# Stationary tiles at other addresses: feed-forward weights in steps of 16 bytes, one buffer of X and of g 64 bytes further

## The chip, the core and the metric

The kernel runs on one core of a Trainium2 chip. The metric is device time in microseconds (us) of one execution. TensorE (PE in the rows) multiplies: a *weight load* (PEld) brings a stationary tile of up to 128 x 128 values from SBUF into the array, and a matmul then streams a moving tile from SBUF through it. VectorE (DVE), ScalarE (ACT) and GpSimd (POOL) do the elementwise work; SyncE (SP) issues transfers.

## The reference, cut to what matters

```python
X = np.fft.rfft(x, axis=1)                         # x: (8, 3072, 256)
Yr = Xr @ w_r - Xi @ w_i + b_r                     # complex channel mixing, 256 x 256
Yi = Xr @ w_i + Xi @ w_r + b_i
Y  = soft_threshold(Yr, 0.01) + 1j * soft_threshold(Yi, 0.01)
y  = np.fft.irfft(Y, n=3072, axis=1)
h  = y.reshape(-1, 256) @ w_in                     # 256 -> 2048
g  = np.where(h >= 1, h, np.where(h <= -1, 0, (h + 1) ** 2 / 4))
out = g @ w_out                                    # 2048 -> 256
```

## The kernel before, in words

Everything is one core's program, written out in a fixed order under `tc.manual_schedule()`; no scheduler moves anything. It has two stages.

**FFT and mixing** (the loop over `u`, 96 steps and a tail). The transform is done by matmuls with tables (`stage1`, `stage2`, `stage3`, `stage4`). The channel mixing between them is L319, `mixed`: the stationary tile is a 128 x 128 piece of X (`Xdh`, `Xdl`, `Xh`, `Xl`: the high and low part of a value, so that three single-pass products stand for one in full precision), the moving tile is a 128 x 256 mixing matrix (`wm_..`). Each step has 18 such matmuls, 96 x 18 = 1,728 in all, and eight steps have 6 more with the narrow `e0` tiles. Each X tile has two buffers, taken in turn from step to step. `stage2` (L251) has `z_first` (first batch) or `zin` (the others) as its stationary tile and the table `t_sb` as its moving one.

**Feed-forward** (the loop over `n`, 256 units; unit n is pair p = n mod 8 of block i = n // 8). In each unit
- L582, `product`, called seven times with three matmuls each: the stationary tile is a 128 x 128 slice of `win` (high or low part, block p), the moving one 128 x 384 of the rows `oph`/`opl`. The seven products are the first matrix product done with seven sub-products in place of eight;
- L638, `down`, eight times with three matmuls each: the stationary tile is a slice of `wout` (block 2p + f), the moving one 128 x 384 of the gated values `gh`/`gl`.

That is 256 x 21 = 5,376 and 256 x 24 = 6,144, together 11,520 matmuls of one form, and runs of `product` and `down` alternate: product 1 and 2, `down` of the unit before last, product 6, `down`, products 5, 7 and 4, `down` of the last unit with f = 1, product 3, `down`, `down` with f = 0. Along this order the stationary tile passes nine times in a unit from one block of weights to another (product to `down`, `down` to product, or from f = 1 to f = 0).

Between these stand `stage4` calls (L500) in every eighth unit, after which the feed-forward stream starts anew.

Where tiles lie: a pool places its tiles one behind the other. Of an address only the remainder modulo 128 bytes is spoken of below. Before the change, each moving tile of L319, L582 and L638 (`wm`, `oph`, `opl`, `gh`, `gl`) and each stationary one (X, `win`, `wout`) begins at a multiple of 128 bytes, and so does each 512-byte row slice of them that one matmul reads, since their sizes are multiples of 128 bytes (`win` of a block 7 x 128 x 4 = 3,584; `wout` of a block 2,048; an X tile 1,024 or 2,048; `g` 3,072). Other remainders occur in the program before in one matmul form that also occurs at remainder 0: `zin` begins 32 bytes past a multiple of 128, `z_first` at a multiple, and `t_sb` at a multiple.

Of the kernel before, what the change touches and what calls it, by code (L numbers as in the profile page):

```python
# [11 lines left out]
F32R = mybir.dt.float32r  # L12
# [4 lines left out]
P = 128  # L17
R1 = 48
R2 = 64
# [84 lines left out]
def tile_fft_mix_moe(  # L104
# [3 lines left out]
    B, S, D = x.shape  # L108
    DFF = w_in.shape[1]
    NF = DFF // P  # L110
    ND = D // P
# [4 lines left out]
    NP = NF // 2  # L116
# [4 lines left out]
    TH = QT * JH // 2  # L121
# [10 lines left out]
    keep = ctx.enter_context(tc.tile_pool(name="keep", bufs=1, side="left"))  # L132
    banks = lambda name: tc.alloc_tile_pool(name=name, bufs=1, space=bass.MemoryType.PSUM, reuse_waits="tile")
    pools = {"ps": banks("psum")}
    dram = ctx.enter_context(tc.tile_pool(name="dram", bufs=1, space=bass.MemoryType.DRAM))
    fold = left("fold")
    mixing = left("mixing")
# [8 lines left out]
    zh, uh = ([a and a.rearrange("(r h) j d -> h r j d", h=2) for a in y_d] for y_d in (z_d, u_d))  # L146


    win = [[keep.tile([P, 7, P], F32R, name=f"win{k}{p}") for p in range(NP)] for k in "hl"]
    z_first = keep.tile([P, G, D], F32, tag="wout", name="z_first")  # L150
    c2_sb = keep.tile([P, R1], F32, name="c2_sb")
    half = keep.tile([P, 1], F32, name="half")
# [20 lines left out]
    def load_x(h):  # L173
        b, m = divmod(h, NJ)
        xin[h] = first_st.tile([P, JT, D], F32, tag="xin", bufs=AHEAD, name="xin")
        if b == 0:
            nc.gpsimd.memset(xin[h][: HP - R1], 0.0)
            to = xin[h][HP - R1 : HP + R1].rearrange("p (a j) d -> p a (j d)", a=2)
            rows = x_first[m].rearrange("a k r i e n -> (k r) a (i e n)")
            for part in (slice(0, 1), slice(1, 2)) if m < 2 else (slice(0, 2),):  # L180
                nc.sync.dma_start(to[:, part], rows[:, part])
            return
        for k in range(2):
            nc.sync.dma_start(xin[h][k * HP : k * HP + R1], xh[b, k, :, m * JT : (m + 1) * JT, :])
# [44 lines left out]
    def store_z(h):  # L229
        b, m = divmod(h, NJ)  # L230
        for k in range(2):
            z = zst.pop((h, k))
            for e in range(2):
                j = m * JT + e * HT
                nc.sync.dma_start(zh[b][k, :, j : j + HT, :], z[e * HP : e * HP + R1])


    zin, xp, dp, yp, over, ust, first_col = {}, {}, {}, {}, {}, {}, {}

    def load_z(u):  # L240
        b, v = divmod(u, NU)
        zin[u] = mixing.tile([P, 2, D], F32, tag="zin", bufs=3, name="zin")
        nc.sync.dma_start(zin[u], zg[b][:, 2 * v : 2 * v + 2, :])
# [15 lines left out]
    def both(ps):  # L259
        return (ps[:, :, c].rearrange("p d g s -> p d (g s)") for c in range(2))  # L260

    def split_X_hi(u):
        ps = xp[u]
        _, im = both(ps)
        if u == 0:
            dp[u] = fold.tile([P, 2, D], F32, tag="yb", name="im")[:, :, :P]
        else:
            dp[u] = mixing.tile([P, ND, P], F32, tag="Xd", name="Xd")
        nc.scalar.copy(dp[u], im)
        if u > 0:  # L270
            round_X(u)

    def round_X(u):
        ps = xp[u]
        hi = mixing.tile([P, ND, 2, 2, R2], F32R, tag="Xh", bufs=2, name="Xh")
        nc.scalar.copy(hi, ps)
        xp[u] = ps, hi

# [28 lines left out]

    def split_difference(u):
        dif = dp[u]
        hi, lo = dp[u] = [mixing.tile([P, ND, P], F32R, tag=f"Xd{k}", bufs=2, name=f"Xd{k}") for k in "hl"]  # L310
        nc.scalar.copy(hi, dif)
        return lambda: nc.vector.tensor_tensor(out=lo, in0=dif, in1=hi.bitcast(F32), op=ALU.subtract)

# [15 lines left out]
    def mix_shared(u):  # L329
        ps = yp[u] = pools["ps"].tile([P, 2, D], F32, tag="C", bufs=2, name="ps_mix")  # L330
        mixed(ps[:, 0, :], [(dp.pop(u), "i")], True)
# [51 lines left out]
    def store_u(u):  # L383
        b, v = divmod(u, NU)
        nc.sync.dma_start(ug[b][:, 2 * v : 2 * v + 4, :], ust.pop(u).rearrange("p k g d -> p (k g) d"))
# [15 lines left out]
    def load_weights(step):  # L401
        if step < NW:
            raw = wraw[step] = first_st.tile([P, WC, 2], U32, tag="wraw", bufs=2, name="wraw")
            nc.sync.dma_start(raw.rearrange("p n k -> p (n k)"), weight_source(step).bitcast(U32))
# [160 lines left out]
    ups, snaps, hs, rs, gs, acc, outs = {}, {}, {}, {}, {}, {}, {}  # L565
# [39 lines left out]
    def of(f):  # L605
        return slice(2 * f, 2 * f + 2)
# [10 lines left out]

    def split_hi(n, f):
        if 0 <= n < NUNIT:
            gs[n, f] = [pools["ffg"].tile([P, 2, TH], F32R, tag=f"g{k}{f}", bufs=2, name=f"g{k}") for k in "hl"]  # L620
            nc.scalar.copy(gs[n, f][0], hs[n][:, of(f)])  # L621

    def split_lo(n, f):
# [52 lines left out]
    def halves(u):  # L676

        lo, hi = (min(NH, NJ + (max(0, k - 1) if k <= NJ else NJ + 2 * (k - NJ) // 3)) for k in (u, u + 1))
        return range(lo, hi)

    def load_t(lo, hi, queue=nc.sync):
        queue.dma_start(t_sb[:, lo:hi, :], t_f[:, lo:hi, :])

    def load_ti(u, queue=nc.sync):
        queue.dma_start(ti_sb[:, u], t_i[:, 2 * u : 2 * u + 2, :])

    with tc.manual_schedule():
# [73 lines left out]
        for u in range(UN + 3):  # L761
            odd = u % 2
            due.extend(h for h in halves(u) if h > NX + 1)
            hs_u = due[: 1 if not odd else max(0, len(due) - 1)]
            del due[: len(hs_u)]
            at = lambda lag: 0 <= u - lag < UN
            weights = more_weights if WU <= u < 85 else lambda: None
            while (stored, 0) in zst:
                store_z(stored)
                stored += 1  # L770
            if at(6) and not odd:
                store_u(u - 6)
            if u == NU:
                wout = keep.tile([P, NF, 2, D], F32R, tag="wout", name="wout")
            if 0 < u < NU - 3:
                load_t(2 * u + 6, 2 * u + 8)
            if 0 < u <= NU:
                load_ti(u - 1)
            if u == WU - 1:
                load_weights(0)  # L780
                load_weights(1)
            if u == 10:
                nc.sync.dma_start(c2_sb, c2)
            if NU <= u + 2 < UN:
                assert stored >= NJ * ((u + 2) // NU + 1)
                load_z(u + 2)
            if xs < min(NH, used + AHEAD):
                load_x(xs)
                xs += 1
            if at(2):  # L790
                mix_shared(u - 2)
            if u == 2:
                take_shared(0)
                split_first(0)
            if at(1):
                difference(u - 1)
                rest = split_difference(u - 1)
                if u == 1:
                    round_X(0)
            if at(2) and u > 2:  # L800
                take_shared(u - 2)
            if at(3):
                above(u - 3)
            if at(1):
                if u > 1:
                    split_X_lo(u - 1)
                rest()
                if u == 1:
                    split_X_lo(u - 1)
                    first_col[0] = minus_sum(*first_col[0])  # L810
                else:
                    split_first(u - 1)
            if at(3):
                shrink(u - 3)
            weights()
            if at(5) and odd:
                stage3(u - 5)
            for h in hs_u:
                stage1(h, "AB", [nc.scalar.copy] * 2)
                used += 1  # L820
            if u in U4:
                half4()
            weights()
            if u == UN + 1:
                half4("DD")
            if u < UN:
                stage2(u)
                split_X_hi(u)
            if u == 1:
                stage1(NX + 1, "AB", [nc.scalar.copy] * 2)  # L830
                used += 1
            if at(2):
                mix_rest(u - 2)
                weights()
                add_bias(u - 2)
            if u == U_IN:
                assert not due and stored == NH
                for _ in ws:
                    pass
                first_st.release()  # L840
                pools["in"] = right("in")
                pools["in"].tile([P, 24], F32, name="edge")
                pools["ops0"] = right("ops0")
                for c in range(2):
                    load_u(c)
            if u == UN - 2:
                prep_sums(0)
            for part in {UN - 2: (0,), UN - 1: (1,), UN: (2, 3)}.get(u, ()):
                prep_split_hi(0, part)
                prep_split_lo(0, part)  # L850
# [24 lines left out]
        for n in range(NUNIT):  # L875
            i, p = divmod(n, NP)
# [24 lines left out]
            if n == 0:  # L901
# [3 lines left out]
                c = next(four4)  # L905
# [24 lines left out]
            if n == 0:  # L930
                c = next(four4)
# [27 lines left out]
            if n in four:  # L959
                c = four[n]  # L960
# [5 lines left out]
        n = NUNIT - 1  # L966
# [41 lines left out]
```

## Time and profile before

| | |
|---|---|
| median of 3 runs | 2570.19 us (2569.08 to 2571.77) |
| the profiled execution's own time | 2569.82 us |
| its span, first to last instruction | 2568.0 us |
| mean granted TensorE clock | 0.999 of full speed (2.4 GHz) |
| busy, share of the span | PE 100%, DVE 80%, ACT 66%, POOL 5% |

Matmuls are pipelined, and a matmul's recorded duration runs on while the next one streams. The pace of a run of matmuls is therefore read from their starts or from the chain (pieces that follow each other, each with its length and count), not from the mean duration.

### The profile page before, as it was taken

The page shows a single profiled execution, that of the slowest core. Times are in us where ns is not written, and L with a number is a line of the kernel's source. Part 1 is how long each engine was busy: PE and PEld are TensorE (multiplying, and loading weights), DVE is VectorE, ACT ScalarE, POOL GpSimd, SP SyncE. Part 2 cuts the span into 40 slices and gives each one's busy share as a digit, 9 for nine tenths or more (in the row PEclk, how much of TensorE's full clock was granted, in tenths as well). Part 3 has the DMA queues.
Part 4 walks back from the last instruction along what each step waited for, and adds up shares of the span by engine and source line. Part 5 has one row for each costly group of instructions (what it writes and reads, how often), then busy time and mean ns, then how long its engine had stood idle before and what let it go on. Part 6 is the DMA issues. An engine that isn't in the chain of part 4 may idle for free.

```text
span 2568.0 us, 48556 instructions
## 1 busy us (share of the span) xinstructions
PE 2557.0 (100%) x19512; PEld 2462.8 (96%) x19512; DVE 2062.4 (80%) x3246; ACT 1693.0 (66%) x2713; POOL 133.4 (5%) x144
## 2 busy tenths in 40 slices
PE   9999999999999999999999999999999999999998
PEld 8888888899999999999999999999999999999998
DVE  5788886688888888888888888888888888888886
ACT  6777776666666666666666666666666666666665
POOL 2243320000000000000000000000000000000000
PEclk9999999999999999999999999999999999999999
DMA  9988775400111111111111111111111111111011
GB/s 245 273 238 240 235 229 157 119 13 13 26 26 26 26 26 26 26 26 24 26 25 25 25 25 25 25 25 25 26 25 25 25 25 25 25 25 25 13 16 22
DMA packets 195345, 160.30 MB, mean 62 GB/s; under 512 B 117296, under 2 KB 167088, under 8 KB 195120
## 3 DMA queue, kind: packets, MB, share of 16 engines
q1 hardware_dynamic: 193312, 156.73, 25.0%
q8 instruction: 153, 2.51, 0.4%
q10 hardware_dynamic: 1808, 0.48, 0.1%
q14 instruction: 72, 0.59, 0.1%
HBM read 84.78 MB, written 72.35 MB: 61 GB/s over the span
## 4 chain that ended last, share of the span: by engine, by line
PE 99%; DVE 0%; ACT 0%; issue 0%
PE acc L638 41%; PE ps_X L582 16%; PE ps_Y L582 10%; PE ps_mix L319 8%; PE ps_Z L582 5%; PE ps_V L582 5%; PE ps_f L251 4%; PE ps_i L367 4%; PE ps_i L500 2%; PE ps_f L217 2%; PE ps_f L195 1%; PE warm L710 0%; DVE h L616 0%; DVE h L601 0%; DVE ot L658 0%
## 5 line engine op out<-in xcount | busy, mean ns | idle before, releaser
L638 PE MATMUL acc<-gh,wout 128*128 128x384 f32 x4096 | 1202.6, 334 | 0.0
L638 PEld LDWEIGHTS acc<-gh,wout 128*128 128x128 f32 x4096 | 754.1, 188 | 0.1
L611 ACT ACTIVATE r<-h,half 128x768 f32<-128x768 f32 x512 | 481.2, 940 | 369.9 <-DVE h L601 369.9
L638 PE MATMUL acc<-gl,wout 128*128 128x384 f32 x2048 | 684.2, 334 | 0.7 <-DVE gl L626 0.7
L626 DVE TENSOR_TENSOR gl<-h,gh 128x768 fp32r<-128x768 f32 x512 | 488.8, 955 | 113.0 <-ACT gh L621 85.1
L595 ACT COPY snap<-ps_X 128x384 f32<-128x384 f32 x768 | 369.2, 481 | 301.7 <-PE ps_X L582 301.5
L616 DVE SCALAR_TENSOR_TENSOR h<-h,r 128x768 f32<-128x768 f32 x512 | 487.0, 951 | 32.1 <-ACT r L611 0.3
L621 ACT CAST gh<-h 128x768 fp32r<-128x768 f32 x512 | 429.8, 839 | 1.5 <-DVE h L616 1.5
L601 DVE CUSTOM_DVE_ANT_0 h<-ps_Y,snap 128x384 f32<-128x384 f32 x512 | 283.5, 554 | 128.7 <-PE ps_Y L582 128.5
L638 PEld LDWEIGHTS acc<-gl,wout 128*128 128x128 f32 x2048 | 384.5, 188 | 0.9 <-DVE gl L626 0.9
L582 PE MATMUL ps_X<-oph,winh 128*128 128x384 f32 x768 | 260.4, 339 | 0.6 <-ACT snap L595 0.6
L582 PE MATMUL ps_X<-oph,winl 128*128 128x384 f32 x768 | 256.8, 334 | 0.0
L582 PE MATMUL ps_X<-opl,winh 128*128 128x384 f32 x768 | 256.6, 334 | 0.0
L601 DVE CUSTOM_DVE_ANT_0 h<-ps_Z,snap 128x384 f32<-128x384 f32 x256 | 142.5, 557 | 104.0 <-ACT snap L595 103.6
L582 PE MATMUL ps_Y<-oph,winh 128*128 128x384 f32 x512 | 171.1, 334 | 0.1
L582 PE MATMUL ps_Y<-oph,winl 128*128 128x384 f32 x512 | 171.0, 334 | 0.0
L582 PE MATMUL ps_Y<-opl,winh 128*128 128x384 f32 x512 | 171.0, 334 | 0.0
L582 PEld LDWEIGHTS ps_X<-oph,winh 128*128 128x128 f32 x768 | 144.1, 188 | 3.6 <-ACT snap L595 1.7
L349 DVE TENSOR_TENSOR y<-ps_mix,shift 128x512 f32<-128x512 f32 x96 | 66.3, 690 | 97.6 <-PE ps_mix L319 97.4
L582 PEld LDWEIGHTS ps_X<-opl,winh 128*128 128x128 f32 x768 | 144.2, 188 | 0.0
L582 PEld LDWEIGHTS ps_X<-oph,winl 128*128 128x128 f32 x768 | 144.2, 188 | 0.0
L601 DVE CUSTOM_DVE_ANT_0 h<-ps_V,snap 128x384 f32<-128x384 f32 x256 | 139.9, 547 | 0.0
(124 smaller groups left out, 3799.5 us busy)
## 6 DMA issues: line engine op xcount, KB each, us to landing
uin<-u_d SPq DMA_DIRECT2D x128, 192.0 KB, 4.0
out<-ot SPq DMA_DIRECT2D x504, 48.0 KB, 2.0
u_d<-ust SPq DMA_DIRECT2D x47, 512.0 KB, 3.7
xin<-in_x SPq DMA_DIRECT2D x112, 192.0 KB, 4.3
z_d<-zst SPq DMA_DIRECT2D x224, 96.0 KB, 2.7
zin<-z_d SPq DMA_DIRECT2D x84, 256.0 KB, 4.0
wraw<-in_moe_w_in SPq DMA_DIRECT2D x16, 256.0 KB, 4.6
wraw<-in_moe_w_out SPq DMA_DIRECT2D x16, 256.0 KB, 4.5
```

The lines of the kernel that those rows point to most:

```text
L251: nc.tensor.matmul(ps[:, d, :, gi, :], lhsT=z[:, gi, d * P : (d + 1) * P], rhs=t_sb[:, 2 * v + gi, :].rearrange("p (c s) -> p c s", c=2), ...
L319: nc.tensor.matmul(out, lhsT=a[:, d], rhs=wm[nm, k][:, d, :], start=start and n == 0, stop=n == 3 * ND * len(pairs) - 1, skip_group_check= ...
L349: nc.vector.tensor_tensor(out=y, in0=yp[u], in1=shift, op=ALU.add)
L367: nc.tensor.matmul(ps[gi][:, k, :], lhsT=ti_sb[rows, v + k, c, :], rhs=y[rows, c, :], start=c == 0 and k == 0, stop=c == 1, tile_position= ...
L582: nc.tensor.matmul(ups[to], lhsT=win[a][p][:, w, :], rhs=mv[:, m, :], start=start and k == 0, stop=k == 2, skip_group_check=True,)
L595: nc.scalar.copy(snaps[n][:, at, :], ups["X"])
L601: nc.vector._custom_dve(TENSOR_ADD_SAT, out=hs[n][:, to, :], in0=ups[a], in1=snaps[n][:, at, :], s0=FLT_MAX, s1=-1.0)
L611: nc.scalar.activation(rs[n][:, of(f)], hs[n][:, of(f)], AF.Square, bias=half, scale=0.5)
L616: nc.vector.scalar_tensor_tensor(out=h, in0=h, scalar=1.0, in1=r, op0=ALU.max, op1=ALU.min)
L621: nc.scalar.copy(gs[n, f][0], hs[n][:, of(f)])
L626: nc.vector.tensor_tensor(out=gl, in0=hs[n][:, of(f)], in1=gh.bitcast(F32), op=ALU.subtract)
L638: nc.tensor.matmul(acc[i, q], lhsT=wout[:, 2 * p + f, a, e * P : (e + 1) * P], rhs=g[:, 1 - t, :], start=p == 0 and f == 1 and k == 0, sto ...
```

## The change

All weights of `win` come into one tile in which each block of 3,584 bytes is followed by 16 unused bytes, and in `wout` each block of 2,048 bytes is followed by 16. So block p of `win` begins at remainder 16 p modulo 128, and block b of `wout` at remainder 16 b (b = 0 to 15). The tiles `Xh`, `Xdh`, `Xdl` and `gh`, `gl` of f = 1 become 64 bytes longer, so that the second of their two buffers begins 64 bytes past a multiple of 128. `Xl` and `g` of f = 0 stay as they are. Tiles that lie behind these move by multiples of 128 bytes, `zin` included in so far as it still begins 32 bytes past one.

The instructions, their shapes, their operands and their order on each engine are the same before and after; only addresses differ (and on VectorE, in the first output of the feed-forward, which of two neighbouring transposes carries the wait for an earlier store).

In numbers of matmuls: of the 11,520 of the feed-forward 7 of 8 (10,080) have their stationary tile at another remainder than before; of the 1,728 of the mixing 672 (14 of 18 in every second step).

```diff
-    win = [[keep.tile([P, 7, P], F32R, name=f"win{k}{p}") for p in range(NP)] for k in "hl"]
+    WIN, STEP = 7 * P, 4
+    win_at = keep.tile([P, 2, NP, WIN + STEP], F32R, name="win")
+    win = [[win_at[:, k, p, :WIN].rearrange("p (w n) -> p w n", n=P) for p in range(NP)] for k in range(2)]
...
+    def spaced(tag, n):
+        return mixing.tile([P, n + 16], F32R, tag=tag, bufs=2, name=tag)[:, :n]
...
-        hi = mixing.tile([P, ND, 2, 2, R2], F32R, tag="Xh", bufs=2, name="Xh")
+        hi = spaced("Xh", 4 * R2 * ND).rearrange("p (d c g s) -> p d c g s", d=ND, c=2, g=2)
...
-        hi, lo = dp[u] = [mixing.tile([P, ND, P], F32R, tag=f"Xd{k}", bufs=2, name=f"Xd{k}") for k in "hl"]
+        hi, lo = dp[u] = [spaced(f"Xd{k}", ND * P).rearrange("p (d n) -> p d n", d=ND) for k in "hl"]
...
-            gs[n, f] = [pools["ffg"].tile([P, 2, TH], F32R, tag=f"g{k}{f}", bufs=2, name=f"g{k}") for k in "hl"]
+            gs[n, f] = [
+                pools["ffg"].tile([P, 2 * TH + 16 * f], F32R, tag=f"g{k}{f}", bufs=2, name=f"g{k}")[:, : 2 * TH].rearrange(
+                    "p (t n) -> p t n", t=2
+                )
+                for k in "hl"
+            ]
...
-                wout = keep.tile([P, NF, 2, D], F32R, tag="wout", name="wout")
+                wout = keep.tile([P, NF, 2 * D + STEP], F32R, tag="wout", name="wout")
+                wout = wout[:, :, : 2 * D].rearrange("p f (a d) -> p f a d", a=2)
```

## Rows read from the trace of the kernel before

**Rows 1.** The page: engines, then the chain's shares by engine and line.
```profile
PE 2557.0 (100%) x19512; PEld 2462.8 (96%) x19512; DVE 2062.4 (80%) x3246; ACT 1693.0 (66%) x2713; POOL 133.4 (5%) x144
PE 99%; DVE 0%; ACT 0%; issue 0%
PE acc L638 41%; PE ps_X L582 16%; PE ps_Y L582 10%; PE ps_mix L319 8%; PE ps_Z L582 5%; PE ps_V L582 5%; PE ps_f L251 4%; PE ps_i L367 4%; PE ps_i L500 2%; PE ps_f L217 2%; PE ps_f L195 1%; PE warm L710 0%; DVE h L616 0%; DVE h L601 0%; DVE ot L658 0%
```

**Rows 2.** Busy time by stretch, in the feed-forward; the first line names the columns.
```profile
core 0: us, PE busy (x) PEld busy (x) DVE busy (x) ACT busy (x) POOL busy (x), PEclk, DMA share, GB/s
1110.00:1160.00 50.00, 50.00 (x290) 49.75 (x289) 41.92 (x61) 32.76 (x48) 0.00 (x0) 1.00 0.11 17
```

**Rows 3.** Chain in order of time, feed-forward: start us, length us, piece, count.
```profile
1101.83 1.56 PE acc L638 x9
1103.38 0.52 PE ps_Y L582 x3
```

**Rows 4.** The mixing: a chain piece, then TensorE's timeline (start us, duration us).
```profile
176.41 2.15 PE ps_mix L319 x18
...
177.69 0.28 PE L319 MATMUL ps_mix<-wm_ih,Xdh 128*128 128x256 f32 x1
...
178.29 0.28 PE L319 MATMUL ps_mix<-wm_ih,Xdl 128*128 128x256 f32 x1
...
181.54 0.28 PE L319 MATMUL ps_mix<-wm_bl,Xh 128*128 128x256 f32 x1
...
182.37 0.28 PE L319 MATMUL ps_mix<-wm_ah,Xl 128*128 128x256 f32 x1
```

**Rows 5.** TensorE's timeline where the feed-forward starts anew, at 1097 us.
```profile
1097.37 0.45 PE L582 MATMUL ps_X<-oph,winh 128*128 128x384 f32 x1
1097.65 0.34 PE L582 MATMUL ps_X<-opl,winh 128*128 128x384 f32 x1
...
1098.54 0.33 PE L638 MATMUL acc<-gh,wout 128*128 128x384 f32 x1
```

**Rows 6.** The same place of the loop at 1032 us.
```profile
1032.74 0.44 PE L582 MATMUL ps_X<-oph,winh 128*128 128x384 f32 x1
1033.02 0.34 PE L582 MATMUL ps_X<-opl,winh 128*128 128x384 f32 x1
...
1033.89 0.33 PE L638 MATMUL acc<-gh,wout 128*128 128x384 f32 x1
```

**Rows 7.** By tile, z_first and zin: count, duration ns min/median/max, first and last start.
```profile
L251 PEld LDWEIGHTS ps_f<-t_sb,z_first x96: 186/192/192, 21.4 to 72.1; 128*128 128x128 f32 x96
L251 PE MATMUL ps_f<-t_sb,z_first x96: 273/275/377, 21.4 to 72.2; 128*128 128x128 f32 x96
...
L251 PEld LDWEIGHTS ps_f<-t_sb,zin x672: 186/192/193, 75.6 to 482.1; 128*128 128x128 f32 x168
L251 PE MATMUL ps_f<-t_sb,zin x672: 270/275/378, 75.6 to 482.2; 128*128 128x128 f32 x168
```

**Rows 8.** By tile, wout and winh: the weight loads, and who writes the tiles.
```profile
L638 PEld LDWEIGHTS acc<-gh,wout x4096: 186/188/189, 506.1 to 2560.4; 128*128 128x128 f32 x196
L442 ACT CAST wout<-both x16: 387/387/390, 248.6 to 392.8; 128x256 fp32r<-128x256 f32 x16
...
L582 PEld LDWEIGHTS ps_X<-oph,winh x768: 186/188/192, 493.7 to 2549.7; 128*128 128x128 f32 x192
...
L464 ACT CAST winh<-wpair x8: 922/922/922, 101.0 to 239.1; 128x896 fp32r<-128x896 f32 x8
L465 POOL TENSOR_TENSOR winl<-wpair,winh x8: 2109/2115/2142, 102.0 to 240.1; 128x896 fp32r<-128x896 f32 x8
```

**Rows 9.** The page, groups by line: busy us, mean ns of one | idle before, releaser.
```profile
L638 PE MATMUL acc<-gl,wout 128*128 128x384 f32 x2048 | 684.2, 334 | 0.7 <-DVE gl L626 0.7
L626 DVE TENSOR_TENSOR gl<-h,gh 128x768 fp32r<-128x768 f32 x512 | 488.8, 955 | 113.0 <-ACT gh L621 85.1
L621 ACT CAST gh<-h 128x768 fp32r<-128x768 f32 x512 | 429.8, 839 | 1.5 <-DVE h L616 1.5
```

## The prediction

> **What bounds the kernel now.** I read the page first: PE is busy for 2557.0 of 2568.0 us, and the chain that ended last is PE for 99%, with nothing waited for [rows 1]. So the time is the sum of what the matmuls take one behind the other, and only their pace counts. Next, the stretches: in 50 us of the feed-forward PE and its weight loads are busy throughout, the granted clock is 1.00, which is the 2.4 GHz level, and VectorE has 8 of 50 us to spare, ScalarE 17 [rows 2]. Then the pace itself, from the chain's pieces. Nine matmuls of the feed-forward take 1.56 us, three take 0.52: 173 ns each [rows 3]. Eighteen of the mixing take 2.15 us, 119 ns each, and inside them the Xd run has five in 0.60 us, 120 ns each [rows 4].
>
> From these two paces follows what there is to win. The feed-forward's matmul has 128 columns more than the mixing's and takes 53 ns more: 0.42 ns a column, one column per cycle at 2.4 GHz. At that rate 384 columns are 160 ns and 256 are 107, so about 13 ns of every matmul of either width are not streaming. Each matmul has a weight load of its own, which runs beside the matmul before it; the 13 ns come with it. Over 11,520 + 1,728 matmuls they are 172 us. The change can act only on these 13 ns, by where the loads read.
>
> **The change part by part.** Nothing is added or removed in instructions, and their order stays.
>
> *Feed-forward weights.* 10,080 of 11,520 matmuls get a stationary tile at another remainder. Does the remainder matter? The trace of before has no single-pass matmul (L319, L582, L638) with a stationary tile off a multiple of 128 bytes, so the cost must be bounded by near rows. The nearest are L251's: the same table `t_sb` moving, the stationary tile once at a multiple of 128 (`z_first`), once 32 bytes past one (`zin`). The loads have 186/192/192 and 186/192/193 ns at least, in the median and at most; the matmuls have 275 ns in the median in both [rows 7]. That a load takes 186 ns at the least and 192 mostly tells that something beside it holds it up, but alike at remainder 0 and 32. I take 0 for this part. These rows are of a two-pass form, whose streaming need not press as hard as the single-pass one, so both ends stay. Downwards: all 13 ns of all 10,080 matmuls, 131 us. Upwards: the slow pace shown below, 5 ns for each of them, 50 us.
>
> There is a second reading of the rows that speaks for a dependence. Where the feed-forward starts anew after `stage4`, the same matmuls in the same order, at the same addresses modulo 128, go at two paces: at 1097 us the five from 1097.65 to 1098.54 take 0.89 us, 178 ns each [rows 5]; at 1032 us the five from 1033.02 to 1033.89 take 0.87 us, 174 ns each [rows 6]. The first matmul of the slow one was 0.28 us long, as was that of the quick one, to within the 0.01 us shown. A few us later the pace is 173 again [rows 3]. So the 13 ns are not a fixed fee: the pace depends on how the load and the stream stand to each other in time, and settles. If it settles by addresses too, other remainders disturb it.
>
> [...]
>
> *X tiles.* 672 of 1,728 mixing matmuls have their stationary tile 64 bytes further. The mixing's own spread bounds this: behind its start, the seven matmuls from 181.54 to 182.37 take 0.83 us, 119 ns, against 120 in the Xd run [rows 4]. One ns more or less for 672 is 0.7 us; even 13 ns would be 8.7. I take 0.
>
> *g tiles.* In every second unit the moving tile of the f = 1 `down` begins 64 bytes further. 128 units x 12 matmuls = 1,536; the stationary ones of these shift anyway, so they are within the first part.
>
> *Writers of the shifted tiles.* `win` and `wout` are written once, by ScalarE (L464, L442) and GpSimd (L465), the last of `win` from 240 us on and of `wout` from 393; the first loads of the feed-forward come at 493 us for `win` and 506 for `wout` [rows 8]. That gap of 100 us and more hides any slower write. `gh` (839 ns, ScalarE) and `gl` (955 ns, VectorE) are written 512 times each, and PE waited for `gl` 0.7 us in all [rows 9]. Steps of 64 bytes leave whole 128 x 768 writes; should each take 1% longer, VectorE's 8 us per 50 cover it. Cost 0. If that cover were gone, 10 ns x 512 would be 5 us.
>
> *The sum.* 0 + 0 + 0 + 0 against the profiled execution's own 2569.82 us (1.8 us more than its span), which stands 0.4 us below the median of 2570.19. Forecast: 2570 us.
>
> **The rivals.**
>
> *Slower: the pace must settle anew at each change of block.* Nine times in a unit the stationary tile passes to another block, and with the change to another remainder: at most 2,304 times in 256 units; before, never. If the pace settles by remainder, each passage is like a start of the stream. A slow start costs 0.02 us more than a quick one (1.17 us against 1.15 from the first matmul to the seventh) [rows 5, 6]. If half the passages are slow, 1,152 x 0.02 = 23 us: 2593 us; if all are, 46 us: 2616. It decides from some 260 slow passages on, which are 5 us. For it: the two paces at starts. Against: the equal rows of `zin` and `z_first`, and that the pace at the two places settles to the same 173.
>
> *Faster: the remainder 0 is what makes load and stream meet.* Then seven of eight blocks go quicker. The trace's nearest quicker row is the mixing's 119 against 120 ns (1.4 ns by 0.83/7 and 0.60/5); that much for 10,080 + 672 matmuls is 15 us: 2555 us. At most it is the whole 13 ns, 131 + 9 us: 2430. It decides when a feed-forward matmul becomes 0.5 ns shorter. For it: the 13 ns are the same in every stretch, as are the remainders, so nothing in this trace has tried others with this form. Against: as above, the `zin` rows, and that no run of feed-forward matmuls settles below 173.
>
> **How the numbers follow.** About 0.2%, 5 us, can be told from no change. I give 0.40 to no effect (2566 to 2575), 0.32 to the slower case (2575 to 2616), 0.28 to the faster one (2430 to 2565). The forecast is the likeliest single case. The range must reach into both others: up to 2612, which leaves out some 0.06 of slower outcomes, and down to 2535, the lower third of the faster case left out, some 0.11. The chances of faster, same and slower are those of the three cases, since each lies on its own side of 5 us.
>
> **What would show it.** Right: pieces of nine `acc` matmuls still 1.56 us, three of any product 0.52, at every p; the loads' median still 188 [rows 8]. The slower case: the 3-pieces just behind a passage grow to 0.53 or 0.54 while later ones of a 9-piece stay at 173 ns. The faster case: pieces below 0.52, and different ones for different p, as each block has its own remainder; p = 0, which keeps remainder 0, is the control within the run. The forecast is wrong if the pace of any block settles away from 173, above all if p = 0 and p = 4 differ.

## The result: slower by 0.8%, inside the range, against the forecast

The median of the changed kernel is 2589.57 us (2589.06 to 2590.0, 4 runs), beside 2569.86 us for the kernel before on the same chip (2569.08 to 2571.77, 4 runs): a ratio of 1.0076, with an interval of 1.0058 to 1.0093. The profiled execution has a span of 2588.2 us against 2568.0 before, so the trace holds 20.2 us to be found.

The page of the kernel after, engines and the chain's shares; in the changed kernel `product` is L587, `down` L648 and the mixing L324:

```profile
PE 2576.2 (100%) x19512; PEld 2481.5 (96%) x19512; DVE 2061.5 (80%) x3246; ACT 1693.1 (65%) x2713; POOL 133.2 (5%) x144
PE 98%; DMA 1%; DVE 0%; ACT 0%; issue 0%; SPq 0%
```

The instruction counts are those of [rows 1]. VectorE, ScalarE and GpSimd are as busy as before, to within 1 us; TensorE alone is longer, by 19.2 us, and the chain is still its work. (The 1% of DMA is the chain's way over the first transfers, in the first 27 us; the FFT stage is not longer.) So no wait was added: the matmuls themselves go slower. Where they do so stands in the weight loads of `down`, by tile `wout`, of the kernel after (duration ns min/median/max, first and last start):

```profile
L648 PEld LDWEIGHTS acc<-gh,wout x4096: 187/188/192, 505.5 to 2580.7; 128*128 128x128 f32 x196
```

From the first to the last of them 2075.2 us pass; before it was 2054.3 [rows 8]. The feed-forward has 20.9 us of the loss, and the stage ahead of it, which ends 0.6 us earlier, none. In the same stretch of 50 us as in [rows 2] the loop moves on by fewer matmuls (287 against 290) at the same granted clock, 1.00:

```profile
1110.00:1160.00 50.00, 50.00 (x287) 50.00 (x286) 42.51 (x62) 33.35 (x49) 0.00 (x0) 1.00 0.10 15
```

And the chain in order of time, pieces of the feed-forward (start us, length us, count):

```profile
1113.97 0.51 PE ps_X L587 x3
1114.48 0.53 PE ps_V L587 x3
1115.01 1.58 PE acc L648 x9
1116.58 0.53 PE ps_Y L587 x3
```

Before, nine `down` took 1.56 us and three matmuls of a product 0.52 [rows 3]. Now nine take 1.58, and pieces of three take 0.51 to 0.53. From the starts of all matmuls, each up to the start of the next one, the products take 946.6 us against 937.2, the `down` 1080.1 against 1068.6, the mixing 222.9 against 223.0. The loss is 1.81 ns on the average of 11,520 matmuls, and no block of the products is free of it: where the stream is not interrupted, p = 0 went from 173.3 to 174.9 ns, p = 4 from 173.3 to 174.5, p = 2 from 173.3 to 175.9. Of the `down`, the f = 0 block of p = 6 hardly lost (173.4 to 173.5), that of p = 4 lost 2.7 ns.

### The profile page after: what moved, and what is told of

The parts are those of the page before. It is cut to its first block, busy times and chain, and to the rows that moved or that the text cites. A ratio compares the mean times of both kernels' runs of the same rounds, so it can differ in the third digit from the quotient of the medians.

```text
span 2588.2 us, 48556 instructions
## 1 busy us (share of the span) xinstructions
PE 2576.2 (100%) x19512; PEld 2481.5 (96%) x19512; DVE 2061.5 (80%) x3246; ACT 1693.1 (65%) x2713; POOL 133.2 (5%) x144
## 4 chain that ended last, share of the span: by engine, by line
PE 98%; DMA 1%; DVE 0%; ACT 0%; issue 0%; SPq 0%
PE acc L648 41%; PE ps_X L587 16%; PE ps_Y L587 10%; PE ps_mix L324 8%; PE ps_Z L587 5%; PE ps_V L587 5%; PE ps_f L253 4%; PE ps_i L372 4%; PE ps_i L505 2%; PE ps_f L219 2%; DMA xin<-in_x 0%; DMA t_sb<-in_t 0%; DMA xin<-in_x_first 0%; DVE h L621 0%; DVE h L606 0%
## 5 line engine op out<-in xcount | busy, mean ns | idle before, releaser
L648 PE MATMUL acc<-gh,wout 128*128 128x384 f32 x4096 | 1214.2, 337 | 0.0
L648 PEld LDWEIGHTS acc<-gh,wout 128*128 128x128 f32 x4096 | 757.7, 188 | 0.1
L648 PE MATMUL acc<-gl,wout 128*128 128x384 f32 x2048 | 691.3, 338 | 0.7 <-DVE gl L636 0.7
L587 PE MATMUL ps_X<-oph,win 128*128 128x384 f32 x1536 | 521.7, 340 | 0.6 <-ACT snap L600 0.6
L648 PEld LDWEIGHTS acc<-gl,wout 128*128 128x128 f32 x2048 | 384.6, 188 | 0.9 <-DVE gl L636 0.9
L587 PE MATMUL ps_Y<-oph,win 128*128 128x384 f32 x1024 | 345.7, 338 | 0.1
L587 PEld LDWEIGHTS ps_X<-oph,win 128*128 128x128 f32 x1536 | 288.4, 188 | 3.5 <-ACT snap L600 1.6
L587 PE MATMUL ps_X<-opl,win 128*128 128x384 f32 x768 | 259.2, 337 | 0.0
L587 PEld LDWEIGHTS ps_Y<-oph,win 128*128 128x128 f32 x1024 | 192.3, 188 | 0.2 <-DVE h L606 0.2
L587 PE MATMUL ps_Z<-oph,win 128*128 128x384 f32 x512 | 172.9, 338 | 0.0
L587 PE MATMUL ps_Y<-opl,win 128*128 128x384 f32 x512 | 172.6, 337 | 0.0
L587 PE MATMUL ps_V<-oph,win 128*128 128x384 f32 x512 | 172.2, 336 | 0.0
L587 PEld LDWEIGHTS ps_X<-opl,win 128*128 128x128 f32 x768 | 144.3, 188 | 0.0
```

Source lines behind the costliest of these rows:

```text
L587: nc.tensor.matmul(ups[to], lhsT=win[a][p][:, w, :], rhs=mv[:, m, :], start=start and k == 0, stop=k == 2, skip_group_check=True,)
L648: nc.tensor.matmul(acc[i, q], lhsT=wout[:, 2 * p + f, a, e * P : (e + 1) * P], rhs=g[:, 1 - t, :], start=p == 0 and f == 1 and k == 0, sto ...
```

## The experiments

Four theories stood at the start or came up.

- **A**, the slower rival of the prediction: the pace settles anew wherever the stationary tile passes to another remainder of 128 bytes, and is undisturbed in between.
- **B**: each remainder of 128 bytes has a pace of its own, whether or not it changes.
- **C**: only the distance between the remainders of the stationary and of the moving tile counts.
- **D**, formed after the bare runs: the pace follows both addresses with a period of 256 bytes, and is lost also where they change within a few matmuls.

### Parts of the change, and a constant remainder

`const16` puts all of `win` and all of `wout` 16 bytes further, with no steps. `win_step` and `wout_step` have the steps of one weight tile alone, `xg_only` the padded buffers of X and g alone.

```diff
-    win = [[keep.tile([P, 7, P], F32R, name=f"win{k}{p}") for p in range(NP)] for k in "hl"]
+    WIN, STEP, SKIP, PART = 7 * P, 0, 4, 0       # const16; win_step: STEP 4, SKIP 0
+    win_at = keep.tile([P, (SKIP + PART + 2 * NP * (WIN + STEP) + 31) // 32 * 32], F32R, name="win")
+    starts = [[SKIP + k * PART + (k * NP + p) * (WIN + STEP) for p in range(NP)] for k in range(2)]
+    win = [[win_at[:, a : a + WIN].rearrange("p (w n) -> p w n", n=P) for a in part] for part in starts]
...
-                wout = keep.tile([P, NF, 2, D], F32R, tag="wout", name="wout")
+                OUT, GAP, SKIP_OUT = 2 * D, 0, 4         # const16; wout_step: GAP 4, SKIP_OUT 0
+                wout = keep.tile([P, (SKIP_OUT + NF * (OUT + GAP) + 31) // 32 * 32], F32R, tag="wout", name="wout")
...
```

> Every block of win and of wout begins 16 bytes past a multiple of 128, at the strides of before; X and g as before. So 11,520 feed-forward matmuls have a stationary tile off the multiple, but no passage along the stream changes the remainder. Theory A (the pace settles anew whenever the remainder of the stationary tile changes): nothing changes along the stream, pieces of nine acc matmuls are 1.56 us again, about 2570 us. Theory B (each remainder has a pace of its own, neighbours or not): all 11,520 go at the pace of the changed kernel's blocks, 2 ns longer or more, pieces of 1.58 us, 2590 to 2600 us. No effect at all of this part: 2570 us with the loss then in X or g.

> Only win is in steps of 16 bytes from block to block; wout, X and g as before. Theory A: a product of block p other than 0 still follows and precedes a down at remainder 0, six or seven passages a unit are left of nine, so both products and downs lose, some 13 to 20 us: 2583 to 2590 us. Theory B: only the products lose, 1.75 ns each as in the changed kernel, 9 us: 2579 us, and acc pieces of nine stay at 1.56 us.

> Only wout is in steps of 16 bytes from block to block; win, X and g as before. Theory A: passages between product and down still change the remainder, and those from f = 1 to f = 0; both lose, 15 to 20 us: 2585 to 2590 us. Theory B: only the downs lose, 1.9 ns each, 11 us: 2581 us, and product pieces of three stay at 0.52 us.

> Only X and g of f = 1 have their second buffer 64 bytes further; the weights as before. Theory A: the passages of 64 bytes in the moving g do not concern the stationary tile; 2570 us, at most 3 us more. Theory B, if only the distance between stationary and moving tile counts: 1,536 downs in 128 units go at another pace, up to 3 us, and the mixing's pieces of eighteen stay within 2.12 to 2.18 us: 2568 to 2574 us.

Beside a median of 2569.14 us for the kernel before:

| | median us | ratio, interval | products us | `down` us | mixing us |
|---|---|---|---|---|---|
| before | 2569.14 | | 937.2 | 1068.6 | 223.0 |
| const16 | 2583.33 | 1.0055 (1.0040 to 1.0070) | 952.7 | 1067.0 | 224.0 |
| win_step | 2589.87 | 1.0081 (1.0064 to 1.0098) | 946.4 | 1080.5 | 223.0 |
| wout_step | 2587.12 | 1.0070 (1.0055 to 1.0085) | 945.2 | 1078.7 | 223.8 |
| xg_only | 2574.26 | 1.0020 (1.0011 to 1.0030) | 937.9 | 1074.2 | 221.7 |

The last three columns are worked out from the starts in each trace. `win_step` and `wout_step` came out in the ranges that A had given, and against B: in `win_step` the `down` lose 11.9 us though their own tiles lie where they lay, and in `wout_step` the products lose 8.0. Two pieces of `down` in the chain of `win_step`, 1.56 before:

```profile
1113.83 1.59 PE acc L641 x9
...
1115.94 1.58 PE acc L641 x9
```

That the parts don't add up, so that the steps of `win` alone or of `wout` alone cost about what all cost together, doesn't speak against A either, since each alone makes most of the passages change. `xg_only` came out a little above what any theory had allowed (A 2573 us, the variant by distance 2574). What does not fit A is `const16`: it has no changing remainder of 128, and its products lose most of all. The chain of `const16`:

```profile
1114.83 1.56 PE acc L641 x9
1116.39 0.53 PE ps_X L585 x3
1116.92 0.53 PE ps_Z L585 x3
```

That seemed to speak for B, but with `win` and `wout` at one and the same remainder of 128, only the products were slow. What had slipped: the size of the `win` tile was rounded to 128 bytes and no further, so that modulo 256 `win` lay at 144 and `wout` at 16.

### Bare runs

To measure the pace by itself, rows of matmuls were put behind the kernel before: each has one weight load per matmul, with a stationary tile of 128 columns and a moving tile read from two copies of the weights at chosen offsets. Behind a first row of 96 matmuls, `pace` has 74 such rows of mostly 48, `pace_fine` 165 of 36 in steps of 16 bytes up to 496. Nothing reads their results, and the times of the whole programs mean nothing here.

```diff
+        def run(count, at_st, at_mv, n=384, cols=P):
+            ps = pools["ps"].tile([P, BANK], F32, tag="pace", bufs=1, name=next(names))
+            for i in range(count):
+                s, m = at_st(i), at_mv(i)
+                nc.tensor.matmul(
+                    ps[:cols, :n], lhsT=st[:, s : s + cols], rhs=mv[:, m : m + n], start=True, stop=True, skip_group_check=True
+                )
...
+        slices, rows = lambda i: i % 6 * P, lambda i: i % 3 * 384
...
+        run(K, lambda i: slices(i) + 4, rows)
...
+        run(K, slices, lambda i: rows(i) + 4)
...
+        run(K, lambda i: slices(i) + 4 * (i % 2), rows)
```

> Behind the unchanged kernel stand 74 runs of 36 to 96 single-pass matmuls more (48 mostly), with nothing to wait for between them and nothing read of their results: weight loads from one tile, streaming from another, at chosen remainders modulo 128 bytes; runs with the two at remainder 0, the loads 16 to 112 bytes further, the streamed tile 16 to 112 further, both further alike, the remainder changing from matmul to matmul, other widths. So the paces alone are measured, about 0.6 ms in all. Theory A (settling, lost only where the remainder changes): every run of constant remainder ends at 173.3 ns a matmul after some five slower ones; runs whose remainder changes every matmul, or every third, stay above, at 175 to 178. Theory B (each remainder of the loads has its own pace): runs of constant remainder 16 differ from 173.3 throughout, by 1.5 ns or more, and the second series of the same remainders gives the same paces as the first. Theory C (only the distance between the two remainders counts): runs with both 16 to 112 further go at 173.3, those with one further do not. In all of them 512 columns should take 53 ns more than 384.

> A second series of bare runs behind the unchanged kernel, 36 matmuls each: at 384 columns the loads 0 to 496 bytes further with the streamed tile fixed, then the streamed tile 16 to 496 bytes further with the loads fixed; the same two series at 256 columns, and one with both moved alike; last the product's own order (high, high, low part of the weights, against high, low, high of the rows) with the loads 256 to 368 bytes further, as in the kernel where they lie 256 bytes off modulo 512. If 128 bytes are the period of the dependence, the paces of the first series repeat after eight steps: 173.3 but for 64 and 80 bytes, again at 192 and 208. If the period is 256 or 512 they do not. If 416 cycles (173.3 ns) are a floor at 384 columns, no run settles below; at 256 columns 288 cycles (120 ns) are no floor, since 284 (118.3) was seen at 16 bytes, and some remainder may go lower still, down to 268 (111.7), the pace of the loads themselves. A pace below 173.3 anywhere would give a version faster than both kernels.

The chain of `pace_fine` shows each row of matmuls as one piece. Here are, at 384 columns, the offsets of before (`ab`), the stationary tile 128 (`aj`), 192 (`an`) and 256 bytes further (`ar`), the moving tile 240 (`bv`) and 256 bytes further (`bw`); then, at 256 columns, the offsets of before (`cm`) and the stationary tile 64 bytes further (`cq`):

```profile
2586.90 6.55 PE pace_ab L998 x36
...
2639.63 6.63 PE pace_aj L998 x36
...
2666.26 6.53 PE pace_an L998 x36
...
2692.73 6.53 PE pace_ar L998 x36
...
2891.28 6.73 PE pace_bv L998 x36
...
2898.05 6.53 PE pace_bw L998 x36
...
3004.12 4.59 PE pace_cm L998 x36
...
3022.47 4.38 PE pace_cq L998 x36
```

Each piece contains its own start, some ten matmuls that are not yet regular (36 x 173.3 ns are 6.24 us, 0.31 less than the piece `ab`). Of the second half of each row the mean pace is, from the starts (ns, offset in bytes from the addresses of before):

| offset | 0 | 16 | 32 | 48 | 64 | 80 | 96 | 112 | 128 | 144 | 160 | 176 | 192 | 208 | 224 | 240 |
|---|---|---|---|---|---|---|---|---|---|---|---|---|---|---|---|---|
| stationary | 173.3 | 173.3 | 173.3 | 173.3 | 174.7 | 176.0 | 173.3 | 173.3 | 176.1 | 177.4 | 176.6 | 173.3 | 173.3 | 175.6 | 176.7 | 173.3 |
| moving | 173.3 | 175.6 | 176.6 | 175.2 | 173.3 | 174.9 | 176.7 | 173.3 | 175.6 | 174.6 | 173.3 | 176.2 | 173.3 | 176.7 | 173.3 | 180.0 |

Offsets from 256 to 496 repeat this table to within 0.1 ns; those from 128 to 240 do not repeat the first eight. So the period is 256 bytes, which B and the prediction had taken as 128. C falls too: both tiles 16 bytes further go at 175.5 ns, both 32 or 64 at 173.3. Where the remainder changes, the pace is lost as A has it, though not only at the passage: the stationary tile at 0 and 16 in turn takes 175.0 ns, three and three 175.5, nine and nine 174.1, while 0 alone and 16 alone take 173.3 each. At all multiples of 128 mixed it takes 174.3, and with the moving tile mixed as well 175.6. The chain of `pace` has 0 alone (`br`), 16 alone (`bs`), the two in turn (`bt`) and three and three (`cc`):

```profile
2953.95 8.61 PE pace_br L998 x48
2962.61 8.61 PE pace_bs L998 x48
2971.26 8.69 PE pace_bt L998 x48
...
3058.22 8.72 PE pace_cc L998 x48
```

This table fits the one part of `xg_only` that I could not place. With f = 1 padded, `gh` and `gl` lie at offsets 0 and 128 in one buffer and at 64 and 192 in the other. The table has 175.6 ns for a moving tile at 128, 173.3 for 0, 64 and 192. In `xg_only` the f = 1 `down` of p = 0, 2, 4, 6 average 175.1 to 175.2 ns, those of p = 1, 3, 5 173.4. The f = 0 `down` of p = 1, 3, 5, 7, whose own tiles did not move, average 174.5 to 175.1. All of that stands in three of their twelve matmuls, the fourth to sixth behind the passage from f = 1, which average 180.7 ns; the other nine are then at 173.2 at the most ((12 x 175.1 - 3 x 180.7) / 9). Why these three are slow stays open.

### Whole kernels by the 256-byte reading

Four kernels test theory D. `same16` is `const16` with tile sizes rounded to 256 bytes, so that `win` and `wout` lie alike modulo 256 and what follows stays. `same128` has 128 bytes in place of the 16. `winlo128` puts only the low parts of `win` 128 bytes further. `x64` moves only the X tiles, all of them by 64 bytes.

```diff
 # same16, same128
+    WIN, STEP, SKIP, PART = 7 * P, 0, 4, 0               # same128: SKIP 32
+    win_at = keep.tile([P, (SKIP + PART + 2 * NP * (WIN + STEP) + 63) // 64 * 64], F32R, name="win")
...
+                OUT, GAP, SKIP_OUT = 2 * D, 0, 4         # same128: SKIP_OUT 32
 # winlo128
+    WIN, STEP, SKIP, PART = 7 * P, 0, 0, 32
 # x64
     e0 = [mixing.tile([P, ND, 32], F32R, name=f"e0{k}") for k in "hl"]
+    mixing.tile([P, 16], F32, name="gap")
...
+        if u == NU:
+            mixing.tile([P, 48], F32, name="gap_z")
         zin[u] = mixing.tile([P, 2, D], F32, tag="zin", bufs=3, name="zin")
```

> Both weight tiles 16 bytes further, each block's step 0, and what follows them at its old remainder of 256: every product and every down reads its stationary and its streamed tile at one constant pair of remainders of 256 (in const16 win lay at 144 and wout at 16, so the pair changed with every switch from products to downs). Theory D (the pace of a row of matmuls follows the two addresses with a period of 256 bytes, as in the bare runs, and it is lost where the remainder changes): the bare runs at 16 bytes settled at 173.33 ns, so products and downs go at 173.3 ns as before and the time is 2570 us within 3. Theory B in its form by 128 bytes (16 bytes off a multiple of 128 is slow by itself, as const16 had it): 2583 us within 3, products at 176 ns or more.

> Both weight tiles 128 bytes further, all the rest where it was (remainders of 256). Period 128: nothing changes, 2570 us. Theory D (period 256): a constant pair that settled at 176.1 ns in the bare runs, 2.75 ns a matmul over 11,520 products and downs is 31.7 us, 2602 us, within 8 since the runs here are shorter than the bare ones; products and downs both at 175 to 177 ns.

> Only the low parts of the feed-forward input weights 128 bytes further, so that the third matmul of each product reads another remainder of 256, but the same of 128. Period 128: 2570 us. Theory D: products lose 1 to 2.7 ns each over 5,376 matmuls (the bare runs with stationary tiles at both remainders took 174.3 ns, those where it changed with each matmul up to 177.5), and downs, which start from an unsettled state, up to 1 ns over 6,144: 5 to 20 us, 2575 to 2590 us.

> Only the tiles of X (Xd and X, both parts, all buffers) 64 bytes further, by a gap ahead of them; zin and all else at their old remainders. Theory D: the bare runs of 256 columns took 120.0 ns at the remainders of before and 113.33 ns with the stationary tile 64 bytes further. 1,728 mixing matmuls by 6.67 ns are 11.5 us: 2558.5 us, 2557 to 2563 with some of it lost to other waits of that stage, and the feed-forward unchanged at 173.3 ns. Rival (the loss comes with any move of addresses away from those of before, or the mixing is not bound by TensorE's pace): 2570 us or more. A period that depended on other things than these remainders would leave mixing at 120 ns.

Beside 2569.25 us for the kernel before:

| | median us | ratio, interval | products us | `down` us | mixing us |
|---|---|---|---|---|---|
| same16 | 2573.40 | 1.0017 (1.0007 to 1.0026) | 938.4 | 1070.2 | 223.3 |
| same128 | 2597.57 | 1.0110 (1.0096 to 1.0124) | 949.8 | 1084.0 | 223.9 |
| winlo128 | 2592.03 | 1.0088 (1.0074 to 1.0102) | 948.0 | 1079.9 | 223.8 |
| x64 | 2562.97 | 0.9979 (0.9970 to 0.9989) | 936.9 | 1068.6 | 216.5 |

Chains of the feed-forward, first `same16`:

```profile
1113.44 0.52 PE ps_Y L585 x3
1113.96 1.56 PE acc L641 x9
```

`same128`:

```profile
1111.10 0.52 PE ps_Y L585 x3
1111.62 1.58 PE acc L641 x9
1113.21 0.53 PE ps_X L585 x3
```

`winlo128`:

```profile
1116.25 0.53 PE ps_V L585 x3
1116.78 1.56 PE acc L641 x9
1118.34 0.53 PE ps_Y L585 x3
1118.86 1.58 PE acc L641 x9
```

`same16` against `const16` takes back 10 of 14 us by nothing but where `wout` and `win` lie modulo 256; nine `down` take 1.56 us and three matmuls of a product 0.52 as before. A rest of some 4 us stays, which puts it 0.4 us above what I had allowed: nearly all its blocks go at 173.6 ns, where before they go at 173.3, and 0.3 x 11,520 are 3.5 us. The bare rows at 16 bytes settled at 173.3, in the kernel's order of high and low parts too; where the 0.3 ns come from stays open.

`same128` and `winlo128` show in whole kernels that the period is not 128 bytes. By 128 bytes nothing changed in either; they lose 28 and 23 us. `same128` is constant throughout and goes at 175.8 ns in nearly every block, beside 176.1 in the bare row. In `winlo128` neither tile of a `down` has moved, and the `down` lose 11.3 us. Its time is 2 us above the upper end of what D expected, because I took at most 1 ns for them and they lost 1.8.

One run shows where the table ends. In `const16` the slow ones are the products, at 176.2 to 176.4 ns, and the quick ones the `down`, at 173.0 to 173.4. By the table it should be the other way about: `win` lies 16 bytes further than before, which settles at 173.3, and `wout` 144 modulo 256, which settles at 177.4. So where the remainder changes every few matmuls, the table does not tell which of them are slow; it has held in the kernels in which each stage keeps one pair of remainders (`same128`, to 0.3 ns `same16`, and in direction though not in size `x64`).

`x64` is the strongest of the four, since it was to gain, in a stage and at a width that the other three leave alone, by a pace read off a bare row of 256 columns. The chain of `x64`, mixing pieces of 18:

```profile
170.60 2.06 PE ps_mix L322 x18
...
174.76 2.06 PE ps_mix L322 x18
...
179.84 2.12 PE ps_mix L322 x18
```

They took 2.15 before [rows 4]. The mixing is 6.5 us shorter, not 11.5: a piece of 18 is two runs, each with an unsettled start, and some pieces gain little. The `down` then start 6 us earlier than in [rows 8] and take as long as they did, 2053.9 us:

```profile
L641 PEld LDWEIGHTS acc<-gh,wout x4096: 186/188/189, 500.1 to 2554.0; 128*128 128x128 f32 x196
```

This version is faster than both kernels: 2562.97 us.

## Why the prediction was wrong, step by step

**What bounds the kernel.** Right: the time is the sum of the matmuls' paces and nothing else, before and after. The 0.42 ns a column held: at the offsets of before, bare rows of 256, 320, 384 and 512 columns settled at 120.0, 146.7, 173.3 and 226.7 ns (448 stood apart, with 206.7 in place of 200.0). That is 2.4 columns in a ns; to call it one column per cycle at 2.4 GHz was my reading, since the traces have the clock only as a share of full speed (1.00 in the stretches of 50 us), and the 13 ns rest on the measured 0.42 ns alone. Where I wrote that the 13 ns come with the weight load, the size of the load has little to do with it: loads of 32 and 64 columns in place of 128 left 384 columns at 173.3 ns, and loads of 96 took 175.0.

**The step that failed** is the first term of the sum, the feed-forward weights, where I took 0 by the rows of `zin` and `z_first`. It measured 20.9 us (the padded g among it), or 1.81 ns for each of the 11,520 matmuls, inside the bounds of 131 us down and 50 us up. The row chosen as the nearest could not show an effect. L251 streams 128 columns at a time, and its matmuls follow each other at 111.6 ns, by their starts, with `z_first` and `zin` alike. At that width the number of columns does not set the pace, as two pieces of the chain of `pace` show, 192 columns (`ci`) and 128 (`cj`):

```profile
3110.65 5.62 PE pace_ci L998 x48
3116.31 5.59 PE pace_cj L998 x48
```

A third fewer columns cost the same, 111.7 ns a matmul once settled; that it is the loads that set it there is my reading. At this pace where the load reads made no difference: in the changed kernel `zin` lies another 128 bytes further modulo 256, a step that at 384 columns leads from 173.3 to 176.6 ns (offsets 32 and 160 of the table), and its matmuls still follow each other at 111.6 ns. At 384 columns the number of columns does count (146.7 ns at 320, 173.3 at 384). And the one step that the row had tried, 32 bytes, is among the nine of 16 that cost nothing at 384 columns either (173.3 ns in the table), so even a row of the right form would have shown no difference there. I had written that the form's streaming need not press as hard, and used the row nevertheless.

**The second reading,** two paces at a start with the same addresses [rows 5, 6], was the row to follow: one and the same stream went at 178 and at 174 ns and settled at 173. I drew from it only the loss at passages. The bare runs add that what it settles to depends on the addresses (173.3 to 180.0 ns at 384 columns).

**Modulo 128.** That p = 0 keeps its remainder and is the control was wrong. In the changed kernel the low part of `win` lies 8 x 16 = 128 bytes off the high part modulo 256, so that even the products of p = 0 change remainder inside one accumulation, and they lost 1.6 ns. For the same reason more tiles had moved than I counted: behind the longer ones `Xl`, `zin` and the first buffer of `gl` (f = 1) lie 128 bytes off their old remainder of 256.

**The slower rival** had 23 us, 3 from what came, and its price per passage is not what was paid. `same128` loses 28 us though no passage in the feed-forward changes the remainder, so passages are not the whole of it; that its 23 us came near is luck. Passages do cost, as nine and nine at 0 and 16 show (174.1 ns, where each alone takes 173.3) and the `down` of `win_step` (11.9 us), so its mechanism is a part of the cause; how much of the 20.9 us is due to passages and how much to slow pairs of remainders no run separates.

**The faster rival.** No bare row of 384 columns with full loads settled below 173.3 ns, stationary or moving, so there was nothing to gain in the feed-forward. At 256 columns there was, 113.3 against 120.0.

**X, g and the writers.** For X I took 0; the mixing lost nothing here and gained 1.3 us in `xg_only`, within the 8.7 us bound. For g, which I put within the first part, `xg_only` has 5.6 us of `down`. The writers cost nothing, as forecast. The page of the kernel after, groups by line:

```profile
L648 PE MATMUL acc<-gl,wout 128*128 128x384 f32 x2048 | 691.3, 338 | 0.7 <-DVE gl L636 0.7
L636 DVE TENSOR_TENSOR gl<-h,gh 128x768 fp32r<-128x768 f32 x512 | 488.6, 954 | 115.6 <-ACT gh L631 87.9
L631 ACT CAST gh<-h 128x768 fp32r<-128x768 f32 x512 | 429.2, 838 | 1.5 <-DVE h L621 1.5
```

Beside [rows 9], `gl` and `gh` take 954 and 838 ns as against 955 and 839, and TensorE waits for `gl` 0.7 us as before.

**The mechanism.** With instructions, shapes and order unchanged, the bare rows of 384 columns settled at anything from 173.3 to 180.0 ns by the two addresses. What makes it so, no run here shows.

## What to carry to other kernels

Where TensorE is the bound and each matmul has its own weight load, where stationary and moving tiles begin was worth from 0.2% gained (`x64`) to 1.1% lost (`same128`) here. Keep the remainders modulo 256 bytes constant along a run, hi and lo parts included, and at a pair that is quick: `same128` kept one and lost most. If padding is needed, multiples of 256 bytes should cost nothing by the bare rows (offsets 256 to 496 have the paces of 0 to 240 to within 0.1 ns); no whole kernel here tried it. To find a better remainder, measure the very shape in bare rows: the stationary tile 16 bytes further leaves 384 columns at 173.3 ns, takes 512 from 226.7 to 233.3 and 256 from 120.0 to 118.3. Then move one family of tiles in the kernel, as `x64` did, since the pace of a row need not be that of the kernel (`const16`). And before a row is used to price an effect, ask what bounds that row: one that is bound elsewhere, as L251 is at 111.6 ns, shows no difference whatever the truth.

## What was not expected of the hardware

- At 384 columns the pace of the bare rows, with a load for each matmul, depended on both addresses with a period of 256 bytes, as measured in steps of 16: of 16 stationary offsets 9 settle at 173.3 ns, of 16 moving ones 6, and the rest up to 180.0. The same rows run a second time in `pace` gave the same pattern (48 matmuls with the stationary tile 80 bytes further took 8.72 us both times, 96 bytes further 8.60).
- At 384 columns 173.3 ns is the lowest to which these rows settle; at 256 columns the lowest is 113.3 ns. At the offsets of before, from 256 to 512 columns, the pace grew by 106.7 ns, 0.417 ns a column; by that rate 384 columns are 160 ns and 256 are 107, so the one lowest pace is about 13 ns above its columns and the other about 7. Why they differ stays open.
- Matmuls whose own tiles did not move became slower beside others whose tiles did: `down` lost 1.9 ns on the average in `win_step` and 1.8 in `winlo128`, where only `win` had moved. In `winlo128` the loss is not spread evenly: of the eight `down` of a unit five stay at 173.3 ns, and three, each right behind a product, take 174 to 181 (the two pieces of nine shown above are 1.56 and 1.58 us for this). The first `down` behind products 5, 7 and 4 stays at 173.3 as well; why, stays open. In `const16` the first `down` behind a product took 170.9 ns, so the average of its `down`, 173.0 to 173.4, is no settled pace below 173.3.
